# Where layer 2's weights are narrowed: eight pieces moved ahead into the retention's units, and later stages for the pieces that are kept

## The chip, the core and the metric

One core of one Trainium2 chip runs the whole program. The metric is the device time in microseconds (us) of one execution. Below, TensorE is the matrix engine (PE in the rows, PEld its weight load), VectorE is DVE, ScalarE is ACT, GpSimd is POOL, and SyncE is SP, whose queue issues nearly all DMAs.

## What is computed

Four batches of 576 tokens go through a retention with eight heads, and its 2304 x 512 result through two feed-forward layers of width 2048.

```python
def _attn_ref(q, k, v):
    scores = scale * np.matmul(q, k.transpose(0, 1, 3, 2))
    Dmat = np.where(rel >= 0, gamma[:, None, None] ** rel[None, :, :], 0.0)
    return np.matmul(scores * Dmat[None, :, :, :], v).astype(np.float32)

def _moe_ref(x, w_in, w_out):        # layer 1
    h = x @ w_in
    return (np.maximum(0.01 * h, h) @ w_out).astype(np.float32)

def _moe2_ref(x, w_in, w_out):       # layer 2
    h = x @ w_in
    return ((h - np.tanh(h)) @ w_out).astype(np.float32)
```

The weights come in float64. The kernel reads them as pairs of 32-bit words and makes float32 of them on the chip.

## The kernel before, in words

**Precision.** Each float32 operand of a product is split in a high and a low half of a reduced type, and a product is three products: high by high, high by low, low by high. `split_into` (line 227) makes the halves: ScalarE copies the high one (228), GpSimd subtracts to get the low one (229).

**Pieces of weights.** `pieces_of` names a piece (layer, kind, f): kind 0 is a part of `w_in`, kind 1 of `w_out`, and there are 16 of each in a layer. `load_piece` (125) is a DMA of 0.52 MB on SP's queue into one of two `stage` buffers. `narrow_ops` (132) makes float32 of it in a buffer `cw`: ScalarE's absolute value (`begin`, 146), then on VectorE the clamp (152), the shift (157) and two joins (163). A piece of layer 1 is then split into its place, `wi` or `wp` (`split_piece`, 217).

**Kept pieces.** Layer 2's pieces are narrowed while layer 1 still runs. `keep_split` (176) splits one into a buffer `sp` (of three) and sends it to DRAM (180); `fetch` (204) brings it back when layer 2 wants it. Layer 2's `w_in` goes through one level of a Strassen-like scheme, so for each pair of pieces of kind 0 `sums_of` (194) forms four sums on VectorE (202), and these are split and kept too. `piece_ops` (479) sets the order: of each piece begin, clamp, shift; then what is left of the piece before it (its split and, for a kept one, DMA, sums and the splits of the sums, all in one go); then the joins and the load of the piece two further on.

**Retention and units.** `retention` runs 16 pairs of heads. From the sixth on, each pair also runs a *unit*: a block of 256 tokens of layer 1's first group by two of its four f (`unit_h`, `unit_o`, 677 and 698). Twelve units are done so. `fill` (664) places the narrowing of group 0's eight pieces among the pairs, by the table `at_pair`; after the eighth pair nothing is left to place.

**Layers.** `layers` runs *steps*: one block of tokens (512, or the one short block of 256) by one f of a group of four. A step is `h_mm` (240, 12 products), the activation `act_a` (315), and `chain` (348), whose GpSimd subtraction (364) makes the low half of `g`; `o_mm` (369) of a step follows two steps later in layer 1 and three in layer 2. A group is 4.5 blocks times four f: 16 long steps and four short ones. During group q of layer 1, `plan` places the narrowing of group q+1's eight pieces and, in groups 1 and 2, of twelve pieces of layer 2; during group 3 those of layer 2's first group. Group q+1's pieces are split in the last steps of group q (`splits`). Then `fold_x` (399) brings layer 1's result into layer 2's form: seven forms for each of three blocks, one a step. In layer 2, two steps are done together (`h_folded`, 253), and what `splits` holds for them comes at the end (926).

The program fixes the order by hand: each engine, and SP's queue, takes its instructions in the order in which the code records them, and one that waits holds all behind it.

Of the kernel before, what the change touches and what calls it, by code (L numbers as in the profile page):

```python
# [10 lines left out]
F32 = mybir.dt.float32  # L11
# [24 lines left out]
def retention_moe_moe(  # L36
# [32 lines left out]
    )  # L69
    narrow = ctx.enter_context(ExitStack())  # L70
    stage = narrow.enter_context(tc.tile_pool(name="stage", bufs=2, side="right"))
# [53 lines left out]
    def load_piece(key):  # L125
        m, kind, f = key
        src = ((w1i, w1o), (w2i, w2o))[m][kind][f]
        st = stage.tile([P, 512], I64 if wide else F32, tag="st", name="st")
        nc.sync.dma_start(out=st, in_=src)
        raw[key] = st  # L130
# [45 lines left out]
    def keep_split(key, wf):  # L176
        sp = pools["sp"].tile([P, 2, 512], F32R, tag="sp", name="sp")
        split_into(sp, wf)
        d = dram.tile([P, 2, 512], F32, tag=f"k{len(kept)}", name="kept")
        nc.sync.dma_start(out=d, in_=sp.bitcast(F32))  # L180
        kept[key] = d

    def keep_ops(key):

        m, kind, f = key
        if kind:
            return [lambda: keep_split(key, half.pop(key))]
        ops = [lambda: keep_split(key, half[key])]
        if f % 2:
            ops += [lambda: sums_of(f - 1)]  # L190
            ops += [lambda j=j: keep_split((j, f - 1), half.pop((1, 0, f - 1 + j))) for j in range(2)]
        return ops
# [39 lines left out]

    def pieces_of(m, g):
        return [(m, kind, g * GF + f) for f in range(GF) for kind in range(2)]


    pools = {}
# [241 lines left out]
    def piece_ops(keys, split=True, spare=()):  # L479


        ops, late = [], []
        for j, key in enumerate(keys):
            part = narrow_ops(key)
            if j + 2 < len(keys):
                part.append(lambda k=keys[j + 2]: load_piece(k))
            ops += part[:3] + late + part[3:]
            late = [lambda k=key: split_piece(k)] if split else []
            if key in spare:
                late = keep_ops(key)  # L490
        return ops + late


    def retention():
        with ExitStack() as ac:
# [163 lines left out]
            ops = piece_ops(pieces)  # L659
            at_pair = [3, 8, 14, 21, 30, 44, 54]  # L660
            first = NP + 1
            done, u = [0], 0

            def fill(i, part):
                a, b = ([0] + at_pair + [len(ops)] * len(order))[i:i + 2]
# [129 lines left out]
    def layers():  # L795
        with ExitStack() as mc:
            pools["t"] = mc.enter_context(tc.tile_pool(name="t1", bufs=2))
            pools["g"] = mc.enter_context(tc.tile_pool(name="g1", bufs=3))
            pools["sp"] = narrow.enter_context(tc.tile_pool(name="sp", bufs=3, side="right"))
# [20 lines left out]
            for q, nxt in zip(groups, groups[1:]):  # L820
                if q[0]:
# [6 lines left out]
                kept_ones = [  # L828
                    (1, kind, f + j)
                    for f in range(GF, NF, 2) for kind in (1, 0) for j in range(2)  # L830
                ]
                a, b = (len(kept_ones) * (q[1] - i) // (NG - 2) for i in (1, 0))
                spare = kept_ones[max(a, 0):b] if 0 < q[1] < NG - 1 else []
# [4 lines left out]
                ops = piece_ops(keys + spare, split=False, spare=spare)  # L838
                plan.setdefault(lo, []).extend([lambda k=k: load_piece(k) for k in (keys + spare)[:2]])
# [22 lines left out]
            for t0, at in ((512, e - 6), (1024, e - 2), (1536, e + 5)):  # L862
                for j, op in enumerate(fold_x(t0)):
                    splits.setdefault(at + j, []).append(op)
# [4 lines left out]
            def due(s):  # L869
                return n_early <= done[0] <= s - lag(s) and done[0] < end - GF  # L870
# [12 lines left out]
            while s < end:  # L883
# [37 lines left out]
                third()  # L921
                o_mm(b, 1)
# [3 lines left out]
                for op in splits.get(s, ()):  # L926
                    op()
# [83 lines left out]
```

## Time and profile before

| | us |
|---|---|
| median of 3 runs | 941.77 (939.63 to 945.75) |
| the profiled execution | 940.31 |
| its span | 938.5 |
| TensorE busy | 874.3 (93%) |
| VectorE busy | 612.7 (65%) |
| GpSimd busy | 488.9 (52%) |
| ScalarE busy | 432.5 (46%) |

The span runs from the first to the last instruction of the profiled execution, which took 1.8 us more than it. A row of the profile gives a line of the kernel, an engine, an operation and what it writes and reads (`out<-in`); the idle time before an instruction stands in brackets, with the engine and line that ended it.

### The profile page before, as it was taken

The page shows a single profiled execution, that of the slowest core. Times are in us where ns is not written, and L with a number is a line of the kernel's source. Part 1 is how long each engine was busy: PE and PEld are TensorE (multiplying, and loading weights), DVE is VectorE, ACT ScalarE, POOL GpSimd, SP SyncE. Part 2 cuts the span into 40 slices and gives each one's busy share as a digit, 9 for nine tenths or more (in the row PEclk, how much of TensorE's full clock was granted, in tenths as well). Part 3 has the DMA queues.
Part 4 walks back from the last instruction along what each step waited for, and adds up shares of the span by engine and source line. Part 5 has one row for each costly group of instructions (what it writes and reads, how often), then busy time and mean ns, then how long its engine had stood idle before and what let it go on. Part 6 is the DMA issues. An engine that isn't in the chain of part 4 may idle for free.

```text
span 938.5 us, 14893 instructions
## 1 busy us (share of the span) xinstructions
PE 874.3 (93%) x5584; PEld 757.9 (81%) x5584; DVE 612.7 (65%) x952; ACT 432.5 (46%) x856; POOL 488.9 (52%) x377
## 2 busy tenths in 40 slices
PE   6779999999979798996989998999999999999997
PEld 5669999888867587775878887888888888888896
DVE  6863433677778577885951477775577657766776
ACT  2333222453343434334432446765555646654663
POOL 4544341372467634677653766745455535554454
PEclk9989999999999799997999998999999999999999
DMA  8733440323564435644640410025001500151211
GB/s 290 235 127 108 148 147 2 112 79 124 195 231 180 157 113 202 224 160 159 215 184 23 145 58 1 1 83 188 1 2 68 202 1 1 46 196 39 76 50 68
DMA packets 35751, 108.82 MB, mean 116 GB/s; under 512 B 4064, under 2 KB 4960, under 8 KB 35680
## 3 DMA queue, kind: packets, MB, share of 16 engines
q1 hardware_dynamic: 35104, 107.49, 33.0%
q8 instruction: 44, 0.72, 0.3%
q10 hardware_dynamic: 576, 0.38, 0.1%
q14 instruction: 27, 0.22, 0.1%
HBM read 77.98 MB, written 29.88 MB: 115 GB/s over the span
## 4 chain that ended last, share of the span: by engine, by line
PE 40%; DVE 9%; POOL 4%; issue 4%; ACT 3%; DMA 1%; POOLq 0%; SPq 0%; ACTq 0%; DVEq 0%
PE a L392 21%; PE h L281 11%; PE h L247 8%; DVE cw L163 2%; DVE acc L455 1%; DVE cw L202 1%; POOL g L364 1%; POOL sp L229 1%; POOL v L336 1%; DVE v L358 1%; DVE v L361 1%; DMA st<-in_w2o 1%; DVE cw L157 1%; DVE xl L470 1%; DVE cw L152 1%
## 5 line engine op out<-in xcount | busy, mean ns | idle before, releaser
L247 PE MATMUL h<-xh,wi 128*128 128x512 f32 (+1 forms) x800 | 231.3, 358 | 0.0
L392 PE MATMUL a<-wp,g 128*128 128x512 f32 x864 | 222.6, 395 | 3.3 <-DVE acc L453 2.5
L392 PE MATMUL a<-g,wp 128*128 128x512 f32 (+1 forms) x816 | 185.1, 375 | 30.5 <-POOL g L364 27.4
L392 PEld LDWEIGHTS a<-g,wp 128*128 128x128 f32 x816 | 145.2, 194 | 60.2 <-POOL g L364 30.4
L392 PEld LDWEIGHTS a<-wp,g 128*128 128x128 f32 x864 | 155.4, 189 | 33.0 <-DVE acc L453 2.9
L247 PEld LDWEIGHTS h<-xh,wi 128*128 128x128 f32 x800 | 144.8, 190 | 23.2
L364 POOL TENSOR_TENSOR g<-v,g 128x512 fp32r<-128x512 f32 (+1 forms) x76 | 99.0, 1303 | 91.0 <-ACT g L363 90.9
L247 PE MATMUL h<-xl,wi 128*128 128x512 f32 (+1 forms) x400 | 143.2, 358 | 0.0
L336 POOL TENSOR_TENSOR v<-t,u 128x512 f32<-128x512 f32 (+1 forms) x76 | 95.2, 1253 | 81.8 <-ACT t L333 78.8
L163 DVE SCALAR_TENSOR_TENSOR cw<-st,cw 128x512 uint32<-128x512 uint32 x128 | 134.4, 1050 | 3.5
L364 POOL TENSOR_TENSOR g<-a,g 128x512 fp32r<-128x512 f32 (+1 forms) x68 | 91.2, 1343 | 52.1 <-ACT g L323 49.5
L229 POOL TENSOR_TENSOR sp<-cw,sp 128x512 fp32r<-128x512 f32 x48 | 69.7, 1458 | 76.0 <-ACT sp L228 48.1
L455 DVE TENSOR_TENSOR acc<-a,acc 128x512 f32<-128x512 f32 (+1 forms) x114 | 69.4, 652 | 33.4 <-PE a L392 33.4
L363 ACT ACTIVATE g<-v 128x512 fp32r<-128x512 f32 (+1 forms) x76 | 45.3, 596 | 97.7 <-DVE v L361 95.1
L152 DVE TENSOR_SCALAR cw<-cw 128x512 f32<-128x512 f32 x64 | 45.5, 711 | 63.3 <-ACT cw L146 62.8
L146 ACT ACTIVATE cw<-st 128x512 f32<-128x512 f32 x64 | 42.9, 672 | 94.3 <-DMA st<-in_w2i 40.8
L358 DVE SCALAR_TENSOR_TENSOR v<-q,v 128x512 f32<-128x512 f32 (+1 forms) x76 | 54.6, 719 | 48.1 <-POOL v L336 48.1
L247 PEld LDWEIGHTS h<-xl,wi 128*128 128x128 f32 x400 | 76.2, 190 | 11.6
L361 DVE COPY_PREDICATED v<-mk,d 128x512 f32<-128x512 uint32 (+1 forms) x76 | 78.8, 1037 | 8.1 <-ACT t L333 0.5
L357 DVE TENSOR_TENSOR d<-h,t 128x512 f32<-128x512 f32 (+1 forms) x80 | 50.8, 635 | 43.1 <-ACT t L333 40.6
L281 PE MATMUL h<-xh,wi 128*128 128x256 f32 x384 | 76.4, 283 | 0.0
L332 ACT ACTIVATE u<-h 128x512 f32<-128x512 f32 (+1 forms) x80 | 44.0, 549 | 63.7 <-DVE h L275 42.4
(84 smaller groups left out, 1310.4 us busy)
## 6 DMA issues: line engine op xcount, KB each, us to landing
kept<-sp SPq DMA_DIRECT2D x48, 512.0 KB, 2.8
wi<-kept SPq DMA_DIRECT2D x32, 512.0 KB, 4.5
st<-in_w1i SPq DMA_DIRECT2D x16, 512.0 KB, 3.5
st<-in_w1o SPq DMA_DIRECT2D x16, 512.0 KB, 3.4
st<-in_w2o SPq DMA_DIRECT2D x16, 512.0 KB, 3.7
st<-in_w2i SPq DMA_DIRECT2D x16, 512.0 KB, 4.1
wp<-kept SPq DMA_DIRECT2D x16, 512.0 KB, 3.7
kv<-in_vn SPq DMA_DIRECT2D x16, 320.0 KB, 4.9
```

The lines of the kernel that those rows point to most:

```text
L152: nc.vector.tensor_scalar(out=wf, in0=wf, scalar1=F64_LO, scalar2=F64_HI, op0=ALU.max, op1=ALU.min)
L163: nc.vector.scalar_tensor_tensor(out=t["w"], in0=t[src], scalar=scalar, in1=t["w"], op0=op, op1=ALU.bitwise_or)
L229: nc.gpsimd.tensor_tensor(out=wp[:, 1, :], in0=wf, in1=wp[:, 0, :].bitcast(F32), op=ALU.subtract)
L247: nc.tensor.matmul(out=ps[:, :n], lhsT=w[:, wi, cs], rhs=x[:, kk, t0:t0 + n], start=kk == 0 and i == 0, stop=kk == KK - 1 and i == 2,)
L281: nc.tensor.matmul(out=out_, lhsT=w[:, wi_, at:at + P], rhs=x(xi, kk), start=start and kk == 0 and j == 0, stop=stop and kk == 1 and j == ...
L336: nc.gpsimd.tensor_tensor(out=v[:, :n], in0=t_[:, :n], in1=u[:, :n], op=ALU.mult)
L357: nc.vector.tensor_tensor(out=d, in0=h, in1=t_, op=ALU.subtract)
L358: nc.vector.scalar_tensor_tensor(out=v, in0=q, scalar=RHO_A, in1=v, op0=ALU.add, op1=ALU.mult)
L361: nc.vector.copy_predicated(out=v, mask=mk.bitcast(U32), data=d)
L364: nc.gpsimd.tensor_tensor(out=gt[:, 1, :n], in0=v, in1=gt[:, 0, :n].bitcast(F32), op=ALU.subtract)
L392: nc.tensor.matmul(out=o, lhsT=l, rhs=r, start=f == 0 and i == 0 and d % pack == 0, stop=f == GF - 1 and i == 2 and (d + 1) % pack == 0, s ...
L455: nc.vector.tensor_tensor(out=dst, in0=a, in1=dst, op=ALU.add)
```

## The change

Four things change.

1. Eight pieces of layer 2, (1, 1, f) for f from 4 to 11 (`early_kept`), are loaded, narrowed, split and kept during the pairs of the retention from the eighth on, beside the units. Groups 1 and 2 of layer 1 then place eight pieces of layer 2 each, where they placed twelve, in another order (all of kind 0 first).
2. A kept piece is split into one of four slots at the start of `wi`, which layer 1 doesn't use, and no longer into a buffer of its own. A piece's split stands where it stood, behind the next piece's shift. What followed it at once is now in stages: the DMA out and the sums come at the end of that next piece, behind its joins and load; the splits of the sums come behind the shift of the piece after it, and their DMAs at its end.
3. In the layers, loads run three pieces ahead through three buffers (`stage1`), which lie on memory that the retention used.
4. `fold_x` of the third block is spread over twelve steps where it took seven, and the forms and fetches of a pair of folded steps' first half come between its two halves of `o_mm`.

```diff
     def keep_split(key, wf):
-        sp = pools["sp"].tile([P, 2, 512], F32R, tag="sp", name="sp")
+        at = len(kept) % 4 * 1024
+        sp = wi[:, at:at + 1024].rearrange("p (i c) -> p i c", i=2)
         split_into(sp, wf)
-        d = dram.tile([P, 2, 512], F32, tag=f"k{len(kept)}", name="kept")
-        nc.sync.dma_start(out=d, in_=sp.bitcast(F32))
+        kept[key] = sp
+
+    def keep_out(key):
+        d = dram.tile([P, 2, 512], F32, tag=f"k{'_'.join(map(str, key))}", name="kept")
+        nc.sync.dma_start(out=d, in_=kept[key].bitcast(F32))
         kept[key] = d
 
     def keep_ops(key):
 
         m, kind, f = key
         if kind:
-            return [lambda: keep_split(key, half.pop(key))]
-        ops = [lambda: keep_split(key, half[key])]
+            return [([lambda: keep_split(key, half.pop(key))], [lambda: keep_out(key)])]
+        stages = [([lambda: keep_split(key, half[key])], [lambda: keep_out(key)])]
         if f % 2:
-            ops += [lambda: sums_of(f - 1)]
-            ops += [lambda j=j: keep_split((j, f - 1), half.pop((1, 0, f - 1 + j))) for j in range(2)]
-        return ops
+            both = [(0, f - 1), (1, f - 1)]
+            stages[0][1].append(lambda: sums_of(f - 1))
+            stages.append((
+                [lambda k=k: keep_split(k, half.pop((1, 0, f - 1 + k[0]))) for k in both],
+                [lambda k=k: keep_out(k) for k in both],
+            ))
+        return stages
 
...
+    early_kept = [(1, 1, f) for f in range(GF, 3 * GF)]
+
...
-    def piece_ops(keys, split=True, spare=()):
-
-
-        ops, late = [], []
+    def piece_ops(keys, ahead=2, split=True, spare=()):
+
+
+        ops, later = [], []
+
+        def due():
+            soon = [x for stages in later for x in stages[:1]]
+            later[:] = [stages[1:] for stages in later if stages[1:]]
+            return [op for x, _ in soon for op in x], [op for _, x in soon for op in x]
+
         for j, key in enumerate(keys):
             part = narrow_ops(key)
-            if j + 2 < len(keys):
-                part.append(lambda k=keys[j + 2]: load_piece(k))
-            ops += part[:3] + late + part[3:]
-            late = [lambda k=key: split_piece(k)] if split else []
+            if j + ahead < len(keys):
+                part.append(lambda k=keys[j + ahead]: load_piece(k))
+            soon, then = due()
+            ops += part[:3] + soon + part[3:] + then
             if key in spare:
-                late = keep_ops(key)
-        return ops + late
+                later.append(keep_ops(key))
+            elif split:
+                later.append([([lambda k=key: split_piece(k)], [])])
+        while later:
+            soon, then = due()
+            ops += soon + then
+        return ops
...
             pieces = split_order(pieces_of(0, 0))
-            ops = piece_ops(pieces)
+            base = len(piece_ops(pieces))
+            ops = piece_ops(pieces) + [lambda k=k: load_piece(k) for k in early_kept[:2]]
+            ops += piece_ops(early_kept, spare=early_kept)
             at_pair = [3, 8, 14, 21, 30, 44, 54]
+            marks = [0] + at_pair + [
+                base + 2 + (len(ops) - base - 2) * i // (len(order) - 7) for i in range(len(order) - 6)
+            ]
             first = NP + 1
             done, u = [0], 0
 
             def fill(i, part):
-                a, b = ([0] + at_pair + [len(ops)] * len(order))[i:i + 2]
+                a, b = marks[i:i + 2] if i < len(order) else marks[-1:] * 2
                 now = a + (b - a) * (part + 1) // 3
                 for op in ops[done[0]:now]:
...
-            pools["sp"] = narrow.enter_context(tc.tile_pool(name="sp", bufs=3, side="right"))
+            pools["st"] = narrow.enter_context(tc.tile_pool(name="stage1", bufs=3, side="right"))
...
                 keys = split_order(pieces_of(*nxt))
                 to_keep = nxt[0] == 1
 
-                kept_ones = [
-                    (1, kind, f + j)
-                    for f in range(GF, NF, 2) for kind in (1, 0) for j in range(2)
-                ]
-                a, b = (len(kept_ones) * (q[1] - i) // (NG - 2) for i in (1, 0))
-                spare = kept_ones[max(a, 0):b] if 0 < q[1] < NG - 1 else []
+                spare = []
+                if 0 < q[1] < NG - 1:
+                    a, b = (len(range(GF, NF)) * (q[1] - i) // (NG - 2) for i in (1, 0))
+                    spare = [(1, 0, f) for f in range(GF, NF)][a:b]
+                    late = [(1, 1, f) for f in range(3 * GF, NF)]
+                    a, b = (len(late) * (q[1] - i) // (NG - 2) for i in (1, 0))
+                    spare += late[a:b]
                 if to_keep:
                     keys, spare = [], [
                         (1, kind, f + j) for f in range(0, GF, 2) for kind in (0, 1) for j in range(2)
                     ]
-                ops = piece_ops(keys + spare, split=False, spare=spare)
-                plan.setdefault(lo, []).extend([lambda k=k: load_piece(k) for k in (keys + spare)[:2]])
+                ops = piece_ops(keys + spare, ahead=3, split=False, spare=spare)
+                plan.setdefault(lo, []).extend([lambda k=k: load_piece(k) for k in (keys + spare)[:3]])
                 free = lo + 11 if to_keep else max(hi if spare else last + 1, lo + 9)
                 span = range(lo + 1, free)
...
             e = per_group[1, 0][0]
-            for t0, at in ((512, e - 6), (1024, e - 2), (1536, e + 5)):
-                for j, op in enumerate(fold_x(t0)):
-                    splits.setdefault(at + j, []).append(op)
+            for t0, at in (
+                (512, range(e - 6, e + 1)), (1024, range(e - 2, e + 5)),
+                (1536, (e + 3, e + 5, e + 7, e + 8, e + 10, e + 12, e + 14)),
+            ):
+                for i, op in zip(at, fold_x(t0)):
+                    splits.setdefault(i, []).append(op)
...
                 act_a(s)
                 o_mm(b, 0)
                 third()
+                for op in splits.get(s, ()):
+                    op()
                 o_mm(b, 1)
                 fourth()
                 act_a(s + 1)
                 chain(s)
-                for op in splits.get(s, ()):
-                    op()
                 assert steps[b][4] != GF - 1
                 for op in splits.get(s + 1, ()):
                     op()
```

How the order of the engines' instructions changes is shown at three places.

GpSimd at the end of layer 1's group 1: `g` is the subtraction of a step's `chain`, `sp` a split of a kept piece of layer 2, `wi` and `wp` splits of group 2's `w_in` and `w_out`. Before:

```order
L229 TENSOR_TENSOR sp<-cw,sp 128x512 x3
L364 TENSOR_TENSOR g<-a,g 128x512
L229 TENSOR_TENSOR sp<-cw,sp 128x512
L229 TENSOR_TENSOR wi<-cw,wi 128x512
L364 TENSOR_TENSOR g<-a,g 128x512
L229 TENSOR_TENSOR sp<-cw,sp 128x512
L229 TENSOR_TENSOR wi<-cw,wi 128x512
L364 TENSOR_TENSOR g<-a,g 128x512
L229 TENSOR_TENSOR sp<-cw,sp 128x512 x4
L229 TENSOR_TENSOR wi<-cw,wi 128x512
L229 TENSOR_TENSOR wp<-cw,wp 128x512
L364 TENSOR_TENSOR g<-a,g 128x512
```

And now, where `wi` is either a kept piece's slot or group 2's `w_in`:

```order
L238 TENSOR_TENSOR wi<-cw,wi 128x512 x2
L374 TENSOR_TENSOR g<-a,g 128x512
L238 TENSOR_TENSOR wi<-cw,wi 128x512
L374 TENSOR_TENSOR g<-a,g 128x512
L238 TENSOR_TENSOR wi<-cw,wi 128x512 x2
L374 TENSOR_TENSOR g<-a,g 128x512
L238 TENSOR_TENSOR wi<-cw,wi 128x512 x4
L374 TENSOR_TENSOR g<-a,g 128x512
L238 TENSOR_TENSOR wi<-cw,wi 128x512 x2
L238 TENSOR_TENSOR wp<-cw,wp 128x512
L374 TENSOR_TENSOR g<-a,g 128x512
```

The bursts of three and four `sp` with sums among them, and the last of them right ahead of group 2's splits, have become bursts of two and four; in both the later ones hold splits of group 2.

SP's queue in group 1, from the first load of layer 2 on (`st` is a load, `kept` a DMA out). Before:

```order
L129 DMA st<-in_w2o 128x512 x2
L129 DMA st<-in_w2i 128x512
L180 DMA kept<-sp 128x1024
L129 DMA st<-in_w2i 128x512
L180 DMA kept<-sp 128x1024
L129 DMA st<-in_w2o 128x512
L180 DMA kept<-sp 128x1024
L129 DMA st<-in_w2o 128x512
L180 DMA kept<-sp 128x1024 x3
L129 DMA st<-in_w2i 128x512
L180 DMA kept<-sp 128x1024
L129 DMA st<-in_w2i 128x512
```

And now, with the loads of all eight pieces and the first three of group 2 at the end:

```order
L130 DMA st<-in_w2i 128x512 x5
L185 DMA kept<-wi 128x1024
L130 DMA st<-in_w2i 128x512
L185 DMA kept<-wi 128x1024
L130 DMA st<-in_w2o 128x512
L185 DMA kept<-wi 128x1024 x3
L130 DMA st<-in_w2o 128x512
L185 DMA kept<-wi 128x1024 x9
L130 DMA st<-in_w1i 128x512 x3
```

The loads stand three pieces further ahead, and of the fourteen DMAs out nine stand behind the last load; before, nearly every load stood behind a DMA out of the piece before it.

VectorE in two pairs of the retention beside units (`cw` is a narrowing, `pt` the mask, `st_104` and `st_105` the states, `xl` the low half of the result). Before:

```order
L613 SCALAR_TENSOR_TENSOR st_104<-st_104,decay,x_c 128x64 x3
L585 SCALAR_TENSOR_TENSOR pt<-sc,cm_sb 128x512 x2
L592 SCALAR_TENSOR_TENSOR pt<-x_a,cm_sb 128x64 x2
L555 TENSOR_TENSOR qk<-qk,qt_sb 128x64
L724 COPY acc<-a 128x2x256
L653 TENSOR_TENSOR xl<-x_c,xh 128x64
L653 TENSOR_TENSOR xl<-o,xh 128x512
```

And now:

```order
L634 SCALAR_TENSOR_TENSOR st_104<-st_104,decay,x_c 128x64 x3
L164 SCALAR_TENSOR_TENSOR cw<-st,cw 128x512
L606 SCALAR_TENSOR_TENSOR pt<-sc,cm_sb 128x512 x2
L613 SCALAR_TENSOR_TENSOR pt<-x_a,cm_sb 128x64 x2
L576 TENSOR_TENSOR qk<-qk,qt_sb 128x64
L153 TENSOR_SCALAR cw<-cw 128x512
L158 TENSOR_SCALAR cw<-cw 128x512
L750 COPY acc<-a 128x2x256
L674 TENSOR_TENSOR xl<-x_c,xh 128x64
L674 TENSOR_TENSOR xl<-o,xh 128x512
```

A clamp and a shift stand behind a pair's mask, and one or two joins ahead of the next one's.

## Rows read from the trace of the kernel before

**Rows 1.** The page: busy us, share of the span, instructions.

```profile
PE 874.3 (93%) x5584; PEld 757.9 (81%) x5584; DVE 612.7 (65%) x952; ACT 432.5 (46%) x856; POOL 488.9 (52%) x377
```

**Rows 2.** TensorE's waits: us in total, times, longest.

```profile
PE a L392 <- POOL g L364: 28.1, 10, 7.3
```

**Rows 3.** Timeline of TensorE, first products of steps: start, us.

```profile
190.07 0.39 PE L247 MATMUL h<-xh,wi 128*128 128x512 f32 x1
...
195.51 0.39 PE L247 MATMUL h<-xh,wi 128*128 128x512 f32 x1
...
351.45 0.28 PE L247 MATMUL h<-xh,wi 128*128 128x256 f32 x1
...
365.57 0.40 PE L247 MATMUL h<-xh,wi 128*128 128x512 f32 x1
...
369.79 0.40 PE L247 MATMUL h<-xh,wi 128*128 128x512 f32 x1
...
527.80 0.40 PE L247 MATMUL h<-xh,wi 128*128 128x512 f32 x1
```

**Rows 4.** Timeline of TensorE, end of group 1; idle before in brackets.

```profile
306.39 0.39 PE L392 MATMUL a<-g,wp 128*128 128x512 f32 x1
313.29 5.06 PE L392 MATMUL a<-g,wp 128*128 128x512 f32 x11 [6.50 <-POOL g L364]
```

**Rows 5.** Timeline of the other engines, same place.

```profile
296.03 1.51 DVE L152 TENSOR_SCALAR cw<-cw 128x512 f32<-128x512 f32 x1
...
297.28 12.64 SPq L180 DMA_DIRECT2D kept<-sp  x5
...
299.01 3.36 DVE L163 SCALAR_TENSOR_TENSOR cw<-st,cw 128x512 uint32<-128x512 uint32 x2
...
302.45 0.63 ACT L228 ACTIVATE sp<-cw 128x512 fp32r<-128x512 f32 x1 [4.46 <-POOL sp L229]
...
304.48 1.80 DVE L202 TENSOR_TENSOR cw<-cw 128x256 f32<-128x256 f32 x4 [2.11 <-POOL sp L229]
...
311.97 1.26 POOL L364 TENSOR_TENSOR g<-a,g 128x512 fp32r<-128x512 f32 x1
...
315.46 0.53 DVE L152 TENSOR_SCALAR cw<-cw 128x512 f32<-128x512 f32 x1 [9.17 <-ACT cw L146]
```

**Rows 6.** Groups by line and form: busy us, mean ns, idle before.

```profile
L163 DVE SCALAR_TENSOR_TENSOR cw<-st,cw 128x512 uint32<-128x512 uint32 x128 | 134.4, 1050 | 3.5
...
L152 DVE TENSOR_SCALAR cw<-cw 128x512 f32<-128x512 f32 x64 | 45.5, 711 | 63.3 <-ACT cw L146 62.8
...
L157 DVE TENSOR_SCALAR cw<-cw 128x512 uint32<-128x512 uint32 x64 | 40.8, 638 | 2.1
...
L229 POOL TENSOR_TENSOR sp<-cw,sp 128x512 fp32r<-128x512 f32 x48 | 69.7, 1458 | 76.0 <-ACT sp L228 48.1 <-issue 20.9 <-PE a L392 6.9
```

**Rows 7.** Timeline of a pair with a unit, retention.

```profile
106.89 0.35 DVE L592 SCALAR_TENSOR_TENSOR pt<-x_a,cm_sb 128x64 f32<-128x64 f32 x2
...
107.56 2.99 PE L709 MATMUL a<-g,wp 128*128 128x256 f32 x24
...
109.81 1.28 POOL L693 TENSOR_TENSOR g<-a,g 128x512 fp32r<-128x512 f32 x1
...
111.39 0.34 PE L643 MATMUL x_c<-pt,kv 128*64 128x64 f32 x4
...
117.15 2.99 PE L709 MATMUL a<-g,wp 128*128 128x256 f32 x24
```

**Rows 8.** Windows: us; busy (instructions) of PE, PEld, DVE, ACT, POOL; PEclk, DMA, GB/s.

```profile
100.00:125.00 25.00, 25.00 (x324) 23.83 (x323) 8.91 (x27) 6.28 (x18) 8.56 (x7) 1.00 0.42 128
...
291.00:320.00 29.00, 21.07 (x80) 16.49 (x79) 17.22 (x19) 13.04 (x24) 23.51 (x17) 0.82 0.42 154
```

**Rows 9.** Timeline of TensorE, layer 2's start.

```profile
564.91 1.42 PE L392 MATMUL a<-wp,g 128*128 128x512 f32 x3 [2.46 <-DVE acc L453]
...
582.26 1.65 PE L281 MATMUL h<-xe,wi 128*128 128x256 f32 x6 [2.47 <-ACT t L290]
```

More of the change, by code (lines that the diff above doesn't have):

```diff
@@ L69, in retention_moe_moe @@
     )
+    pools = {}
     narrow = ctx.enter_context(ExitStack())
-    stage = narrow.enter_context(tc.tile_pool(name="stage", bufs=2, side="right"))
+    pools["st"] = narrow.enter_context(tc.tile_pool(name="stage", bufs=2, side="right"))
     qb = keep.tile([P, 4], F32, name="qb")
@@ L127, in load_piece @@
         src = ((w1i, w1o), (w2i, w2o))[m][kind][f]
-        st = stage.tile([P, 512], I64 if wide else F32, tag="st", name="st")
+        st = pools["st"].tile([P, 512], I64 if wide else F32, tag="st", name="st")
         nc.sync.dma_start(out=st, in_=src)
@@ L231, in split_into @@
         )
+    early_kept = [(1, 1, f) for f in range(GF, 3 * GF)]
     def pieces_of(m, g):
         return [(m, kind, g * GF + f) for f in range(GF) for kind in range(2)]
-    pools = {}
     hp, ga, tmp, ac_ps = {}, {}, {}, {}
```

## The prediction

> **What bounds the kernel now.** I read the busy totals first. TensorE is busy for 93% of the span [rows 1], so the gain of any edit is bounded by the time in which TensorE stands or runs slowly. The waits of TensorE say for whom: 28.1 us in ten waits for GpSimd's subtraction that makes the low half of `g` (line 364) [rows 2]. The long ones lie in layer 1, as the one of 6.50 us at its second group's end [rows 4].
>
> How much that stretch loses is counted by steps. A quiet step of 512 tokens takes 195.51 - 190.07 = 5.44 us [rows 3]. A group is 4.5 blocks of four steps, so 18 x 5.44 = 97.9 us, and a little more, since a short block is worth more than half a long one: from 351.45 to 369.79 four short steps and the long one behind them take 18.3 us; with the next, again about 4.2, that is 22.5 for six steps that count as four, so 0.8 more. Groups 1 to 3 need 3 x 98.7 = 296.1 us and took 527.80 - 190.07 = 337.7 [rows 3]. **41.6 us** are lost there. They are the waits and what follows them: after the wait of 6.50 us eleven products take 5.06 us [rows 4], where twelve take 2.72 when quiet (half a step), so they ran at the lower of the two clock levels (1.2 against 2.4 GHz); the granted clock of that stretch is 0.82 [rows 8].
>
> Why `g` is late is read at the end of group 1 from the timeline of the other engines [rows 5]. VectorE takes 1.51 us for a clamp and 3.36 for two joins. ScalarE stands 4.46 us in front of a split until the join is done, and behind that split, on the same queue, is the next step's activation. VectorE stands 2.11 us in front of the sums for GpSimd's half of the split that was issued just ahead of them. GpSimd then has four `sp` splits and two of the next group ahead of `g`, which starts at 311.97. SP's queue holds five DMAs for 12.64 us, each until its split is done; the next group's loads are behind them, and VectorE stands 9.17 us for the first of these. So it is a chain of short waits, each of an engine in order for a piece that is not ready. It is not throughput alone: between 291 and 320 us VectorE is busy 17.22 of 29 us and GpSimd 23.51 [rows 8].
>
> **The change part by part.** *Eight pieces leave layer 1.* A narrowing costs VectorE 0.711 + 0.638 + 2 x 1.050 = 3.45 us, and each split of a kept piece costs GpSimd 1.458 [rows 6]. Groups 0 to 3 of the code narrow 8, 20, 20 and 8 pieces before; now 8, 16, 16 and 8. Groups 1 and 2 lose 4 x 3.45 = 13.8 us of VectorE and 5.8 of GpSimd each, of 97.9. The sums stay at three pairs in each.
>
> *Sums and DMAs come later.* A split stands where it stood, behind the next piece's shift. But the sums and the DMA out, which followed it at once, now follow the next piece's joins and load, and the splits of the sums another piece later. So GpSimd's split has the time of two joins (2.1 us) before VectorE asks for it, and the wait of 2.11 goes; a late split holds no load on SP's queue. The last piece of groups 1 and 2 was of kind 0, whose join, split, sums and splits of the sums ran one behind the other with nothing between (the 4.46 and the 2.11 us of [rows 5]); now pieces of kind 0 come first and two of kind 1 last, so that the sums' splits lie beside a narrowing. *Loads three ahead* with three buffers give a load one more piece, some 4 us, where ScalarE and so the clamp at 315.46 waited for a load [rows 5]. All this is one answer, since each wait feeds the next: I take the 41.6 as recoverable, less what GpSimd's queue keeps. At the end of group 1 four splits and then three still stand between two `g`. With 1.458 a split and 1.26 for `g` that is 7.1 us, then 5.6, against a step of 5.44. A `g` has about one step of slack, so the first is covered and the second may be late by some 2 us. For two group ends and the sums inside the groups I leave **6 us** of the 41.6. Bounds: 0 left if the slack holds, 21 if both group ends stay (one costs 6.50 + 5.06 - 2.5 = 9.0 us in group 1 [rows 4]; I take as much for group 2, and 3 for the rest).
>
> *Eight pieces enter the units.* There TensorE is busy without a gap and a pair takes 117.15 - 107.56 = 9.59 us [rows 7]; VectorE is busy 8.91 of 25 us, ScalarE 6.28 and GpSimd 8.56 [rows 8]. VectorE's share of a pair is 3.4 us; 3.45 more leaves 2.7 free. Up to two joins now stand ahead of the mask: 2.1 us, or 3.36 at worst [rows 5, 6]. The mask ends at 107.24 and TensorE needs `pt` at 111.39, so 4.15 us cover them [rows 7]. GpSimd's `g` ends at 111.09 and is needed at 117.15, 6 us later; one split is 1.458. If a cover failed, each of eight pairs would pay about 1 to 3 us, 8 to 24 in all; I take 1.5 us for the first and last pair. The DMAs out there are issued a pair after their split, so the next pair's loads don't wait for them. The traffic, eight loads and eight stores of 0.52 MB, falls on some 85 us, which is 99 GB/s beside the 128 GB/s that hold a DMA share of 0.42 [rows 8]; both together stay below the whole.
>
> Beside this: the Trainium skill (SBUF — State Buffer, "SBUF: two separate sides") says that GpSimd and a VectorE operation with two SBUF inputs or in a two-port mode take turns on one port pair, one fully blocking the other. The trace agrees in kind: one clamp took 0.53 us and another, with GpSimd busy throughout, 1.51 [rows 5]. By that rule a moved piece may cost VectorE 1.51 + 1.51 + 3.36 = 6.4 us, which with 3.4 exceeds a pair's 9.59 by 0.2; the sum would rise by 8 x 0.2 = 2 us.
>
> *The first loads of the layers* now wait for memory that the retention gave back, where before only the narrowed pieces did. Three are issued together, and the first narrowings have a whole group 0 in front of their use. I cost it at 0; 3 us if ScalarE is held by the first.
>
> *Layer 2's start.* TensorE waits 2.46 us for an accumulator and 2.47 for ScalarE's copy [rows 9]. The second stands behind two `fold_x` forms in one pair of steps, and now only one stands there, so it goes, with the slower products after it: **3 us**. The first waits behind VectorE's own chain and stays. Bounds 0 and 6.
>
> **Sum.** 940.3 us (the profiled execution: span 938.5 and 1.8 around it) - (41.6 - 6) - 3 + 1.5 = 903.2. That run lies 1.5 us below the median of the three, so I put **904 us**.
>
> **Rivals.**
> (a) *The group ends stay.* GpSimd is the busiest of the three there and still has the next group's eight splits in four steps. If its queue, not the chain, makes `g` late, 21 us of the 41.6 remain: 904 + 15 = 919 us. For it: 23.51 of 29 us busy [rows 8]. Against it: the waits of ScalarE and VectorE in [rows 5] are for each other's unready pieces, and they go.
> (b) *The units pay.* The gain in layer 1 comes, but moved work makes each of eight pairs 3 us longer, since TensorE has no gap there: 904 + 24 = 928 us. Against it: the covers of 4.15 and 6 us.
> (c) *Slots run short, slower than before.* Kept splits go to four slots in `wi`, and a slot is written again only when its DMA has left. If SP's queue stands in front of a load, the DMA behind it starts late and ScalarE stops at the split, with the activations behind it. There are three bursts of three splits in each of two groups and as many single ones between: 12 places. It decides once each costs over 4 us (12 x 4 = 48 is more than the 36 gained, plus 1%): about 952 us. Against it: a slot comes back four splits, so more than a piece, later.
> (d) *Nothing moves:* the waits are made by the order of `g` itself and only change their releaser: 940 us. Against it: where pieces are narrowed and none is kept, steps are quiet (190.07 to 195.51 [rows 3]).
>
> **How the numbers follow.** I give 904 us (897 to 911) 0.6, the best bounds (891 to 897) 0.05, (a) 0.18, (b) 0.07, (c) 0.05 and (d) 0.05. The range 892 to 926 leaves out (c), (d), most of (b) and a little of the best bounds; 1 in 100 of (b) lies above 932. About 1% is what a measurement here can tell from no change. Faster by over 1% (below 932): 0.89; within 1%: 0.06; slower: 0.05.
>
> **What would show it.** Right: groups 1 to 3 take about 302 us from their first product to layer 2's; waits of TensorE for `g` fall below 8 us; VectorE no longer waits for GpSimd ahead of the sums, and ScalarE hardly for loads; pairs stay at 9.6 us. Wrong: pairs above 10 us (b); waits for `g` only at the two group ends (a); splits waiting for DMAs (c).

## The result, and the profile after

The changed kernel takes **905.55 us** (median; 903.76 to 906.04), the kernel before beside it 940.7: a ratio of 0.9619, 95% interval [0.9571, 0.9668]. The forecast was 904 in 892 to 926. Its profiled execution spans 904.1 us, the page's busy row:

```profile
PE 864.4 (96%) x5584; PEld 751.8 (83%) x5584; DVE 615.6 (68%) x952; ACT 431.3 (48%) x856; POOL 489.6 (54%) x377
```

Against [rows 1] TensorE does as many products in 9.9 us less (874.3 to 864.4; the granted clock of the whole run went from 0.976 to 0.989, so fewer of them ran at the lower of its two levels) and idles 24.5 us less. Together that is the 34.4 us by which the span fell. By place (first products of groups, counted as in [rows 3]): group 1 starts 1.0 us later (190.07 to 191.07), groups 1 to 3 take 303.1 us in place of 337.7 (-34.6), layer 2 takes 409.9 in place of 410.7 (-0.8).

The waits after (engine, what waits, for whom: us in all, times, longest), in which line 392 of before is now 402, 364 is 374, 202 is 211 and 146 is 147:

```profile
PE a L402 <- POOL g L374: 5.8, 5, 3.8
...
PE a L402 <- DVE acc L463: 2.5, 1, 2.5
```

The first answers to [rows 2]: 28.1 us fell to 5.8. Among the waits of the other engines, VectorE's for GpSimd ahead of the sums fell from 11.8 us to 1.2, and ScalarE's for loads from 90.8 us to 2.8. Before, and after:

```profile
DVE cw L202 <- POOL sp L229: 11.8, 7, 2.4
```

```profile
ACT cw L147 <- DMA st<-in_w2o: 2.4, 1, 2.4
```

Groups 1 and 2 are now quiet: 98.7 us each, the figure that the prediction gave for a group without loss, in place of 108.2 and 116.1. Group 3 takes 105.8 in place of 113.4. Of the 7.1 us that it still loses, some 5.6 stand at one place: a wait of 3.80 us and eleven products in 4.26 that take about 2.5 when quiet. TensorE, then GpSimd, ScalarE and VectorE in front of it (start, us; idle before in brackets):

```profile
446.46 4.26 PE L402 MATMUL a<-g,wp 128*128 128x512 f32 x11 [3.80 <-POOL g L374]
```

```profile
440.39 4.79 POOL L238 TENSOR_TENSOR wi<-cw,wi 128x512 fp32r<-128x512 f32 x3 [6.16 <-ACT wi L237]
445.15 1.26 POOL L374 TENSOR_TENSOR g<-a,g 128x512 fp32r<-128x512 f32 x1
```

```profile
438.38 1.41 ACT L471 ACTIVATE xh<-acc 128x256 fp32r<-128x256 f32 x4 [4.35 <-DVE acc L465]
439.70 1.66 ACT L237 ACTIVATE wi<-cw 128x512 fp32r<-128x512 f32 x3
```

```profile
433.10 2.40 DVE L164 SCALAR_TENSOR_TENSOR cw<-st,cw 128x512 uint32<-128x512 uint32 x2
435.42 1.79 DVE L211 TENSOR_TENSOR cw<-cw 128x256 f32<-128x256 f32 x4
...
437.93 1.41 DVE L465 TENSOR_TENSOR acc<-a,acc 128x256 f32<-128x256 f32 x4
```

Read it from the bottom. VectorE does two joins and four sums before it adds a finished block (line 465). ScalarE, in order, stands 4.35 us for that block with three splits of kept pieces behind it. GpSimd so gets its three halves in one burst and reaches `g` at 445.15, too late for TensorE. Only in group 3, the last of layer 1, does a block end also make the halves of layer 2's input (lines 471 and 480).

### The profile page after: what moved, and what is told of

Read it like the earlier page. It is cut to its first block, busy times and chain, and to the rows that moved or that the text cites. A ratio compares the mean times of both kernels' runs of the same rounds, so it can differ in the third digit from the quotient of the medians.

```text
span 904.1 us, 14903 instructions
## 1 busy us (share of the span) xinstructions
PE 864.4 (96%) x5584; PEld 751.8 (83%) x5584; DVE 615.6 (68%) x952; ACT 431.3 (48%) x856; POOL 489.6 (54%) x377
## 4 chain that ended last, share of the span: by engine, by line
PE 77%; DVE 11%; POOL 4%; ACT 3%; issue 3%; DMA 1%; SPq 0%; POOLq 0%; DVEq 0%; ACTq 0%
PE a L402 33%; PE h L257 21%; PE h L291 11%; PE a L735 4%; PE x_b L710 3%; DVE cw L164 3%; DVE acc L465 1%; DVE v L368 1%; PE o L652 1%; PE sc L591 1%; POOL v L346 1%; PE o L664 1%; DVE v L371 1%; DVE cw L158 1%; DVE cw L153 1%
## 5 line engine op out<-in xcount | busy, mean ns | idle before, releaser
L402 PE MATMUL a<-g,wp 128*128 128x512 f32 (+1 forms) x816 | 178.0, 367 | 4.7 <-POOL g L374 4.4
L402 PEld LDWEIGHTS a<-g,wp 128*128 128x128 f32 x816 | 142.2, 190 | 30.7 <-POOL g L374 5.0
L374 POOL TENSOR_TENSOR g<-v,g 128x512 fp32r<-128x512 f32 (+1 forms) x76 | 98.7, 1299 | 94.7 <-ACT g L373 94.6
L164 DVE SCALAR_TENSOR_TENSOR cw<-st,cw 128x512 uint32<-128x512 uint32 x128 | 138.4, 1081 | 3.7
L238 POOL TENSOR_TENSOR wi<-cw,wi 128x512 fp32r<-128x512 f32 x64 | 91.1, 1437 | 68.8 <-ACT wi L237 58.7
L374 POOL TENSOR_TENSOR g<-a,g 128x512 fp32r<-128x512 f32 (+1 forms) x68 | 88.1, 1299 | 64.3 <-ACT g L333 62.2
L332 ACT ACTIVATE a<-h 128x512 f32<-128x512 f32 (+1 forms) x68 | 37.2, 547 | 168.8 <-PE h L257 156.4
L371 DVE COPY_PREDICATED v<-mk,d 128x512 f32<-128x512 uint32 (+1 forms) x76 | 81.6, 1074 | 7.8
```

Source lines behind the costliest of these rows:

```text
L164: nc.vector.scalar_tensor_tensor(out=t["w"], in0=t[src], scalar=scalar, in1=t["w"], op0=op, op1=ALU.bitwise_or)
L238: nc.gpsimd.tensor_tensor(out=wp[:, 1, :], in0=wf, in1=wp[:, 0, :].bitcast(F32), op=ALU.subtract)
L371: nc.vector.copy_predicated(out=v, mask=mk.bitcast(U32), data=d)
L374: nc.gpsimd.tensor_tensor(out=gt[:, 1, :n], in0=v, in1=gt[:, 0, :n].bitcast(F32), op=ALU.subtract)
L402: nc.tensor.matmul(out=o, lhsT=l, rhs=r, start=f == 0 and i == 0 and d % pack == 0, stop=f == GF - 1 and i == 2 and (d + 1) % pack == 0, s ...
```

## The experiments

Two theories. **Chain**, the prediction's: the short waits feed each other, and later stages (a kept piece's sums and DMAs recorded later) with loads three ahead take them away; four narrowings fewer in a group are a small help. **Load**: VectorE and GpSimd had too much to do in groups 1 and 2, and the waits go because the move takes 13.8 and 5.8 us a group away. All edits are against the changed kernel, three rounds each. The kernel before had a median of 939.7 beside e1 to e4, 941.9 beside e5 to e9 and 942.0 beside e10 to e13, so medians are compared closely only within these sets.

| run | us | ratio, 95% interval | groups 1, 2, 3 (us) |
|---|---|---|---|
| changed kernel | 905.55 | 0.9619 [0.9571, 0.9668] | 98.7, 98.7, 105.8 |
| e1 no move | 920.93 | 0.9802 [0.9776, 0.9828] | 103.2, 108.1, 107.4 |
| e2 no later stages | 906.75 | 0.9654 [0.9628, 0.9679] | 100.0, 99.6, 104.6 |
| e3 loads two ahead | 910.99 | 0.9700 [0.9668, 0.9732] | 100.7, 99.7, 108.8 |
| e4 both of these | 914.91 | 0.9738 [0.9705, 0.9771] | 103.9, 99.6, 109.2 |
| e8 as e4, kind 0 last | 914.53 | 0.9717 [0.9702, 0.9732] | 98.7, 102.5, 110.6 |
| e9 as e4, no move | 934.55 | 0.9940 [0.9917, 0.9962] | 108.9, 113.2, 109.7 |
| e5 folds back | 907.74 | 0.9645 [0.9630, 0.9661] | 98.7, 98.7, 105.8 |
| e6 their place alone | 906.35 | 0.9626 [0.9608, 0.9644] | 98.7, 98.7, 105.5 |
| e10 VectorE's work back | 915.13 | 0.9711 [0.9697, 0.9726] | 102.8, 102.1, 108.5 |
| e11 GpSimd's work back | 909.99 | 0.9659 [0.9639, 0.9679] | 100.6, 99.5, 106.0 |
| e12 twelve pieces moved | 901.82 | 0.9566 [0.9541, 0.9590] | 98.7, 99.7, 99.1 |
| e13 group 3 spread | 905.10 | 0.9601 [0.9587, 0.9616] | 98.7, 98.7, 105.3 |

### The move, the stages and the loads

**e1**, twelve kept pieces in each of groups 1 and 2 again, with stages and early loads:

```diff
...
-            ops += piece_ops(early_kept, spare=early_kept)
...
-                    late = [(1, 1, f) for f in range(3 * GF, NF)]
+                    late = [(1, 1, f) for f in range(GF, NF)]
```

> The changed kernel, but no piece of layer 2 is narrowed beside the units: groups 1 and 2 of layer 1 keep twelve pieces each as before, of kind 0 first. Stages, slots in `wi`, loads three ahead and the folds stay. If a chain of short waits made `g` late, which the stages cut, most of the 34 us stays: 915 to 922 us, with groups 1 and 2 at 98.7 us plus at most 8 each. If it was VectorE's load, which only the move lowers, the stalls come back: 930 to 938 us, groups 1 and 2 at 108 to 113.

**e2**, in the layers a kept piece's sums, splits and DMAs at once, as before:

```diff
...
+            while at_once and later:
+                more, after = due()
+                soon, then = soon + then + more, after
...
```

> The changed kernel, but in the layers a kept piece's split, DMA out, sums, splits of the sums and their DMAs are recorded at once behind the next piece's shift, as before the change. The move to the units, the order of kinds, the slots and the loads three ahead stay. If the chain made `g` late, about half of the gain goes: 915 to 925 us, with waits of TensorE for `g` of 3 to 7 us at the sums. If VectorE's load did, nothing changes: 903 to 908.

**e3**, loads two ahead and two buffers in the layers:

```diff
-            pools["st"] = narrow.enter_context(tc.tile_pool(name="stage1", bufs=3, side="right"))
...
-                ops = piece_ops(keys + spare, ahead=3, split=False, spare=spare)
+                ops = piece_ops(keys + spare, ahead=2, split=False, spare=spare)
...
```

> The changed kernel, but loads in the layers run two pieces ahead through the two buffers of the retention. If late loads held ScalarE, and so the activations behind it, 908 to 915 us, with ScalarE's waits for loads back at some 60 us. If they only cost time that no one waits for, 904 to 907.

**e4** has the edits of e2 and e3 together.

> The changed kernel with both e2's and e3's edits: only the move of eight pieces, the order of kinds, the slots and the folds are left. If the load of VectorE is the cause, 904 to 909 us. If the chain is, 918 to 930 us: worse than with either edit alone, since late DMAs out then hold the loads again.

**e9** has the edits of e4 and of e1: what is left of the change is the order of kinds, the slots in `wi` and the folds.

> The kernel of e4 without the move: groups 1 and 2 keep twelve pieces each, at once and with two loads ahead, but those of kind 0 first. If the order of kinds made most of e4's gain, 918 to 925 us, without long waits at the ends of groups 1 and 2. If the load of VectorE did, near the kernel before: 933 to 940.

Without the move 15.4 us come back (e1). Later stages and early loads without the move, e9 to e1, are worth 13.6, and with it, e4 to the changed kernel, 9.4 (across sets, and so good to some 2 us). The move without them, e9 to e4 and e8, is worth 19.6 to 20.0, the largest single part. Of the 9.4, the loads carry more than the stages: e3 loses 5.4, with 38.2 us of ScalarE's waits for loads back, e2 only 1.2; the rest shows only where both are missing. Yet e2 brings the waits back that the prediction's chain was read from (first e2, then the changed kernel):

```profile
ACT wi L237 <- DVE cw L211: 26.7, 8, 3.9
...
DVE cw L211 <- POOL wi L238: 11.0, 6, 3.8
```

```profile
ACT wi L237 <- DVE cw L211: 3.8, 4, 1.6
```

That is 37.7 us of waiting in place of 5.0 (3.8 and 1.2), and the 32.7 us more cost about 1 us.

Neither theory has it all. e2 and e9 came out where the load was expected to put them (903 to 908, 933 to 940), but e1, at 920.9, where the chain was (915 to 922, against 930 to 938), and e4, at 914.9, in neither range (904 to 909, 918 to 930).

**e8**, e4 with kind 1 first and kind 0 last:

```diff
...
-                    spare = [(1, 0, f) for f in range(GF, NF)][a:b]
+                    early = [(1, 0, f) for f in range(GF, NF)][a:b]
...
-                    spare += late[a:b]
+                    spare = late[a:b] + early
```

> The kernel of e4 (eight pieces moved, work of a kept piece at once, two loads ahead) with the kept pieces of groups 1 and 2 in the old manner: kind 1 first, so that a pair of kind 0 with its sums comes last. If the end of a group is late because join, split, sums and splits of the sums run one behind the other there, the stalls of some 9 us at both group ends come back: groups 1 and 2 longer by 12 to 18 us together, 927 to 933 us. If only VectorE's load counts, as e4: 912 to 918.

The time is that of e4 (914.5 and 914.9), so with eight kept pieces in a group the order of kinds is worth nothing; with twelve it was not tried alone. It does set the place of the waits. In the last step of groups 1 and 2, where the kernel before waits 6.50 [rows 4] and 7.31 us, e8 waits

```profile
300.74 2.81 PE L402 MATMUL a<-g,wp 128*128 128x512 f32 x11 [2.26 <-POOL g L374]
...
402.60 2.79 PE L402 MATMUL a<-g,wp 128*128 128x512 f32 x11 [1.61 <-POOL g L374]
```

and e4 not at all; e4 waits 2.39 us in the middle of group 1.

### VectorE's and GpSimd's load, each alone

**e10** does three joins again for four kept pieces in each of groups 1 and 2 (25.2 us by the mean join of [rows 6], in all; VectorE's busy time in the two groups grew by 14.8):

```diff
...
+            if key in spare and key[1] == 0 and GF <= key[2] and key[2] % 3:
+                part += [part[3], part[4], part[4]]
```

> The changed kernel, with VectorE's work put back and nothing else: four of the kept pieces in each of groups 1 and 2 have their joins done again (three joins of 1.05 us each, which write the same bits), 12.6 us of VectorE a group where the move took 13.8 away. No load, no split and no DMA is added. If it was VectorE's load that made groups 1 and 2 late, they lose most of the 15.4 us by which the changed kernel without the move is longer: 915 to 921 us, groups 1 and 2 at 102 to 108 us in place of 98.7. If it was the number of splits, loads and DMAs in the queues (the chain of unready pieces), nothing waits for these joins and the time stays within 2 us of 905.6.

**e11** does GpSimd's half of four splits again in each (11.7 us in all):

```diff
...
+        if len(key) == 3 and key[1] == 0 and GF <= key[2] and key[2] % 3:
+            nc.gpsimd.tensor_tensor(
+                out=sp[:, 1, :], in0=wf, in1=sp[:, 0, :].bitcast(F32), op=ALU.subtract
+            )
```

> The changed kernel, with GpSimd's work put back and nothing else: four kept pieces in each of groups 1 and 2 have the subtraction of their split done twice (the same bits), 4 x 1.46 = 5.8 us of GpSimd a group, as much as the move took away. If the length of GpSimd's queue in front of g was what the move shortened (rival a's engine), groups 1 and 2 go from 98.7 to 102 or more each and the time to 912 to 921 us. If it was VectorE's load, GpSimd has room for it: within 2 us of 905.6.

The spans grow by 10.3 us (904.1 to 914.4) and 3.0 (to 907.1), the medians by 9.6 and 4.4. Neither adds a load, a DMA or a piece, and ScalarE's waits for loads stay short in e10 (4.9 us, 2.8 in the changed kernel), so VectorE's load by itself makes `g` late: the first theory's answer for e10 (within 2 us) fell. e11 came out between its two answers (within 2 us, or 912 to 921): GpSimd's work counts, for less than was expected, and VectorE's busy time grew with it by 8.3 us, so what GpSimd's own queue costs is not separated. The sum of the two, 14.0 us by the medians, is near the 15.4 that e1 loses, but it is no account of them: e10 gave VectorE 14.8 us in groups 1 and 2, e1 27.6. Busy time from the first product of group 1 to that of group 3, in the changed kernel, e4, e11, e10, e1 and the kernel before (us; PE, PEld, DVE, ACT, POOL; PEclk, DMA, GB/s):

```profile
191.07:388.44 197.37, 197.37 (x962) 167.18 (x960) 151.44 (x197) 83.29 (x160) 113.39 (x82) 1.00 0.46 155
```

```profile
192.81:396.36 203.55, 199.81 (x962) 168.21 (x960) 146.19 (x198) 82.37 (x157) 111.45 (x82) 0.99 0.42 153
```

```profile
191.32:391.35 200.03, 198.29 (x961) 166.90 (x960) 159.69 (x197) 83.54 (x160) 126.25 (x90) 1.00 0.45 153
```

```profile
191.05:395.92 204.87, 200.27 (x961) 167.79 (x960) 166.24 (x221) 82.08 (x157) 111.81 (x81) 0.99 0.44 147
```

```profile
190.19:401.46 211.27, 203.17 (x961) 170.68 (x960) 179.05 (x227) 91.52 (x173) 129.16 (x91) 0.98 0.53 184
```

```profile
190.07:414.38 224.31, 204.87 (x962) 171.23 (x961) 172.46 (x223) 90.33 (x170) 123.44 (x88) 0.96 0.49 171
```

Divide VectorE's busy time by 2 x 98.7 = 197.4 us: the share that it would have if TensorE lost nothing. With stages and early loads it is 77% in the changed kernel, which loses nothing; 81% in e11 (2.6 us lost), 84% in e10 (7.5) and 91% in e1 (13.9). GpSimd's share does not line up so: 57%, 64%, 57% and 65%. No engine is full, yet the loss grows with VectorE's share. The share is not the whole answer: without the stages and early loads e4 loses 6.2 us at 74%, and the kernel before, with its own order too, 26.9 at 87%. One such place in e10, VectorE, GpSimd and TensorE:

```profile
253.36 1.79 DVE L211 TENSOR_TENSOR cw<-cw 128x256 f32<-128x256 f32 x4
...
255.98 8.52 DVE L164 SCALAR_TENSOR_TENSOR cw<-st,cw 128x512 uint32<-128x512 uint32 x5
```

```profile
255.89 4.69 POOL L238 TENSOR_TENSOR wi<-cw,wi 128x512 fp32r<-128x512 f32 x3 [3.01 <-ACT wi L237]
260.54 3.41 POOL L374 TENSOR_TENSOR g<-a,g 128x512 fp32r<-128x512 f32 x2
```

```profile
262.32 4.12 PE L402 MATMUL a<-g,wp 128*128 128x512 f32 x10 [2.14 <-POOL g L374]
```

VectorE's sums end late, so three splits come to GpSimd at once; beside five joins they and `g` run slower (1.70 us a `g`, 1.26 at 445.15 above), and TensorE stands 2.14 us and then takes 4.12 for ten products, 2.3 when quiet. The links are those that the prediction named; what feeds them here is load. Of the 10.3 us that e10's span grows by, 2.7 fall in group 3, which has no added join; what carries them there is not shown.

### Layer 2's folds, and group 3

**e5** puts the last fold's steps back to one after the other, and the splits behind the chain; **e6** only the second:

```diff
...
-                (1536, (e + 3, e + 5, e + 7, e + 8, e + 10, e + 12, e + 14)),
+                (1536, range(e + 5, e + 12)),
...
-                for op in splits.get(s, ()):
-                    op()
                 o_mm(b, 1)
                 fourth()
                 act_a(s + 1)
                 chain(s)
+                for op in splits.get(s, ()):
+                    op()
```

> The changed kernel with the folds of the third block in seven steps in a row again, and the forms and fetches of a folded pair at its end, as before the change. If the folds gave 3 us of the gain, 907 to 910 us, with the wait of 2.5 us for ScalarE's copy back. The traces of before and after differ by only 0.8 us in layer 2: by them 905 to 907.

> The changed kernel with only the place of the forms and fetches in a folded pair put back to its end; the third block's folds stay spread. If the place between the halves of `o_mm` costs what the spread gives (a wait of 1.03 us for ScalarE's evacuation, which the kernel before did not have), 902.5 to 905 us. If the place gives the gain, 906 to 909.

In e5 TensorE's wait for ScalarE's copy is back at 1.71 us, and layer 2 takes 411.0 us against 409.9; e6 is not told from the changed kernel. The folds are worth 1 to 2 us.

```profile
548.58 0.97 PE L291 MATMUL h<-xe,wi 128*128 128x256 f32 x6 [1.71 <-ACT t L300]
552.12 0.95 PE L291 MATMUL h<-xe,wi 128*128 128x256 f32 x6 [1.18 <-DVE mk L285]
```

**e12** moves group 3's four pieces of kind 1 to the units too; **e13** gives group 3's eight pieces thirteen steps in place of ten:

```diff
...
-    early_kept = [(1, 1, f) for f in range(GF, 3 * GF)]
+    early_kept = [(1, 1, f) for f in range(3 * GF)]
...
-                        (1, kind, f + j) for f in range(0, GF, 2) for kind in (0, 1) for j in range(2)
+                        (1, kind, f + j) for f in range(0, GF, 2) for kind in (0,) for j in range(2)
```

```diff
...
-                free = lo + 11 if to_keep else max(hi if spare else last + 1, lo + 9)
+                free = lo + 14 if to_keep else max(hi if spare else last + 1, lo + 9)
```

> The changed kernel with twelve pieces in the units: the four of kind 1 that group 3 narrows go there too, so group 3 keeps four in place of eight. If the 7 us left in group 3 are the load of its ten steps, as in groups 1 and 2 before, group 3 falls from 105.8 to 99 or 100 us and the time to 899 or 900. If the units have no room for a third more (rival b: VectorE then has 3.4 + 1.5 x 3.45 = 8.6 of a pair's 9.59 us), each of eight pairs is 1 to 3 us longer: 907 to 923 us.

> The changed kernel with group 3's eight kept pieces spread over thirteen steps in place of ten, with no other difference. If the 7 us left in group 3 come of how densely the pieces stand there, most of it goes: 899 to 902 us. If they come of the one place where the last sums and their splits meet the splits of the last narrow weights, that place only moves three steps later, beside the first fold of layer 2's input, and the time stays within 2 us of 905.6 or gets longer.

e13 changes nothing; its longest wait for `g` only sits at another block end, behind the same queue:

```profile
426.31 2.72 PE L402 MATMUL a<-g,wp 128*128 128x256 f32 x11 [3.27 <-POOL g L374]
```

e12 takes four of the pieces away, and group 3 falls to 99.1. It is the fastest run, 901.8 us. Between 100 and 190 us TensorE is busy for 88.44 us there, in the changed kernel for all 90.00: the units begin to pay. Two waits, each alone, can be read: 0.46 us for ScalarE's half of `g`, and, ahead of the layers' first product, 1.06 us for a half of the retention's result.

## Why the prediction was right, and where not

**The total.** 904 against 905.55: right, and groups 1 to 3 at 303.1 us against "about 302". The signs named came: waits for `g` at 5.8 us (below 8), hardly a wait ahead of the sums or for loads, pairs at 9.59 us. That it lies so near is in part luck: the size of the main term was right for a reason that was in part wrong, and of the small ones the units cost less than was put down and layer 2 gave less.

**"All this is one answer."** This step failed in its reason. It gave the 13.8 us of VectorE and 5.8 of GpSimd that leave a group no price of their own, and put the gain on stages and loads. The runs show the move as the largest part (15 to 20 us by what it is taken from). Loads and stages together are worth 9 to 14; taken out alone, the loads are worth 5 and the stages 1. The sentence "it is not throughput alone" rested on 17.22 of 29 us busy [rows 8]; but that stretch holds VectorE's stall of 9.17 us itself. Over groups 1 and 2 VectorE had 172.46 us to do in the 197.4 that TensorE needs: 87%.

**"The last piece was of kind 0"**, as a cause of late group ends: right for the place and not for the price. With kind 0 last the waits stand at the two group ends again (e8), but it is as fast as e4.

**The 6 us left.** The size was right by luck (7.0 us over 3 x 98.7), for the place was not. Nothing is left at the ends of groups 1 and 2, which GpSimd's splits and `g` were to make late by 2 us. All of it is in group 3, which the prediction counted as fully recoverable without a look at its kept pieces beside the block ends.

**The units, 1.5 us,** and the first loads of the layers, put at 0: no cost is seen. Pairs stay at 9.59 us, and TensorE is busy for all of the 90 us between 100 and 190 before and after, though VectorE's busy time between 100 and 125 us went from 8.91 [rows 8] to 16.64. That group 1 starts 1.0 us later tells nothing: it starts at 190.1 to 192.8 us in the runs with eight pieces in the units, and at 190.1 to 190.9 in those with none. e12 has 20.86 there:

```profile
100.00:125.00 25.00, 24.54 (x317) 23.18 (x317) 20.86 (x42) 11.68 (x30) 15.41 (x11) 1.00 0.80 262
```

VectorE at 83% costs TensorE 0.46 us in these 25, where 87% in the layers went with 26.9 us lost in two groups. Why is not shown. The covers of 4.15 and 6 us [rows 7] are a reason, but a `g` in the layers has about one step, 5.44 us, so the size of the slack alone does not tell the two apart. The 2 us that the sum would have risen by the rule of the Trainium skill (SBUF — State Buffer, "SBUF: two separate sides") did not come. Between 100 and 190 us VectorE has 28 instructions more, seven pieces, and 23.3 us more to do: 3.3 us a piece, near the sum's 3.45. The 6.4 us a piece that the prediction worked out by that rule did not come either.

**Layer 2's start, 3 us.** Over-sized: 0.8 in the profiles, 1 to 2 by e5. The wait of 2.47 us [rows 9] fell to 0.33 and the one of 2.46 stayed, as said. But others took its place: 1.22 us for VectorE's `mk` (all such waits: 2.5 us before, 3.2 after) and 1.03 for ScalarE's copy of a block, which had none.

```profile
546.77 0.97 PE L291 MATMUL h<-xe,wi 128*128 128x256 f32 x6 [0.33 <-ACT t L300]
550.63 0.96 PE L291 MATMUL h<-xe,wi 128*128 128x256 f32 x6 [1.22 <-DVE mk L285]
572.27 0.96 PE L402 MATMUL a<-wp,g 128*128 128x512 f32 x3 [1.03 <-ACT acc L461]
```

**The rivals.** (a) fell: no wait is left at the two group ends. GpSimd's load did count (e11), as a part. (b) and (d) fell with the pairs and the time. (c): no split waits for a DMA in the changed kernel; in e1, with twelve pieces a group, one does, for 4.3 us. That the slots would run short with fewer of them was not tried.

```profile
POOL wi L238 <- DMA kept<-wi: 4.3, 1, 4.3
```

**Open:** what in e9 makes the 6 us by which it beats the kernel before (order of kinds, slots in `wi`, folds); the folds account for 1 to 2.

## What to carry to other kernels

Price a move by the load that it takes from the stretch where the bound engine waits: divide an engine's busy time there by the time that the bound engine needs without a stall, and expect losses long before 100% (here from 81% on, and from 74% without the stages or the early loads). Long waits of engines off the path can cost next to nothing (32.7 us more of them cost 1 here), so a chain of waits tells how lateness travels, not what it costs. A busy share alone does not price the place that the work goes to: the retention took it at 67% for nothing and at 83% for little.

## What the hardware showed

A join has not one duration but, in the main, two. The groups of the changed kernel and of e11 by line (ns: min/median/max):

```profile
L164 DVE SCALAR_TENSOR_TENSOR cw<-st,cw x128: 672/693/1823, 15.5 to 442.4; 128x512 uint32<-128x512 uint32 x128
```

```profile
L164 DVE SCALAR_TENSOR_TENSOR cw<-st,cw x128: 676/908/1821, 16.0 to 445.8; 128x512 uint32<-128x512 uint32 x128
```

In the changed kernel 71 of the 128 joins take less than 0.72 us, 45 take 1.5 or more and 12 lie between. All 53 that run while GpSimd does nothing take 0.68 to 0.70 us, and each of the 57 above 0.8 runs beside a GpSimd instruction. So the mean of 1.05 us in the prediction's sum is a mixture, and the median of e11 jumps because 64 of its joins are slow where 57 were. In e11 VectorE is busy for 159.69 us in groups 1 and 2 in place of 151.44, for the same 197 instructions: eight more GpSimd subtractions (11.7 us) cost VectorE 8.3.

The Trainium skill (SBUF — State Buffer, "SBUF: two separate sides") says that the two engines share one port pair as a lock, not as a share of bandwidth; for VectorE that holds where an operation has two SBUF inputs, as a join has, or runs in a two-port mode. The trace agrees in kind: 1.82 - 0.69 = 1.13 us is most of one GpSimd subtraction of 1.26. The two clamps that the prediction set side by side (0.53 and 1.51 us) do not show it, for GpSimd worked beside both (a split from 314.42 to 315.71 us, and `g` from 315.66); the joins do. So work added to GpSimd was paid by VectorE too. The other way round nothing shows: in e10 GpSimd takes 111.81 us for 81 instructions and in the changed kernel 113.39 for 82, 1.38 us each.
